# Storing the masked x^T phi(k) wv so that each product's 32 stationary columns are adjacent

## The chip, the core and the metric

The kernel runs on one core of a Trainium2 chip. Its engines are TensorE (PE in the profile; PEld is its weight load), VectorE (DVE), ScalarE (ACT), GpSimd (POOL) and SyncE (SP), which issues most DMAs. The metric is the device time of one execution in microseconds.

## The reference

Two linear-attention blocks, A and B, read the same input `x` (2048 x 640) with weights of their own, and a sigmoid gate per row mixes their outputs. There are 32 heads of 20 columns.

```python
qkv = (x @ wqkv) split into q, k, v, each (32 heads, 2048, 20)
phi = lambda t: jnp.where(t > 0, t + 1, jnp.exp(t)) + 1e-6
pq, pk = phi(q), phi(k)
kv  = einsum("bhsd,bhse->bhde", pk, v)
z   = einsum("bhsd->bhd", pk)
num = einsum("bhqd,bhde->bhqe", pq, kv)
den = einsum("bhqd,bhd->bhq", pq, z)[..., None] + 1e-6
block = (num / den, heads side by side) @ wo
g   = sigmoid((x * gate_w).sum(-1))
out = g * block_A + (1 - g) * block_B
```

## The kernel before

The kernel does not form v. Since kv = phi(k)^T x wv, it first computes G = x^T phi(k) (640 x 640), then wv^T G for four heads at a time, keeps what belongs to equal heads, and multiplies that by wo. The result is a matrix M per block (640 x 640), with which the output is phi(q) M, summed over both blocks after phi(q) has been scaled by gate and denominator.

The order of the work, all of it on TensorE with DVE and ACT behind:

- phi(k) of A in 16 row chunks (`k_chunk`, matmuls L205) mixed with half of phi(q) of A (`q_block`, L265), then the rest of phi(q) (`q_unit`, L254), the gate and the sums of phi(k).
- G of A (`g_pass`, L288, and `g_strassen`, L315), into the tiles `GT` (written by L285, L344, L332 and L362).
- phi(k) of B (16 chunks). After the second of them comes `kvt_pass(0)`: the 40 matmuls of wv^T G (`kvt_mm`, L396) and the masks (`kvt_mask`, L403) for A. After four of the later chunks DVE also takes a difference of rows (`p_diff`).
- phi(q) of B in ten units. `m_unit(0, c, "act")`, the wo product of A for one of five column sets c, stands after the first unit (c = 0), and in pairs after two later ones. Its matmuls are L429, and ACT copies the result to `M[0]` (L274).
- G of B, again by `g_pass` and `g_strassen`.
- The end, in an order written out by hand: `kvt_mm(1, kv, 0)`, `kvt_mask(kv, 0)`, `pairs[0].p1()` (five matmuls L515), `kvt_mm(1, kv, 1)`, `kvt_mask(kv, 1)`, row sums of phi(q) on DVE (`p_sums`, L454), `pairs[1].p1()`, and then the five wo products of B (L429) with sums of M on DVE between them (`m_sums`, L454).
- The output in eight pairs of row tiles (`Pair`, seven products in place of eight, matmuls L515, DVE additions L520), each stored by a DMA of SP.

Around the change: `KVT` holds, for each of four groups g, three stretches of 80 columns. The first and the third take the masked product of two sets of four heads; the middle one stays zero from a single memset (L105). `maskE` (80 x 80) is one where row and column belong to the same head. A wo product (`m_half`) runs four matmuls at a time, one for each g in its own 32 columns of the array (`tile_position`), for k = 0 and then k = 1. Its stationary operand has 80 rows and 32 columns: of two neighbouring stretches, every fifth column from c on (`mixed(heads, c)`). 16 of them come from masked data and 16 from zeros, so that k = 0 fills the first 16 rows of the result and k = 1 the last 16. In the order of memory the columns are thus 5 elements, 10 bytes, apart. Each `m_unit` has 16 such matmuls of 320 moving columns.

The code of these pieces runs under a manual schedule, so each engine's instructions stand in the order in which the program names them; the semaphores follow from which tile is read and written.

Of the kernel before, what the change touches and what calls it, by code (L numbers as in the profile page):

```python
# [8 lines left out]
P = 128  # L9
FP32 = mybir.dt.float32  # L10
BF16 = mybir.dt.bfloat16
ACT = mybir.ActivationFunctionType
ALU = mybir.AluOpType
# [3 lines left out]
DT = D // P  # L17
# [4 lines left out]
HF = D // 2  # L22
TW = 4
KG = 80
# [7 lines left out]
def kernel(  # L32
# [11 lines left out]
    nc = tc.nc  # L44
# [4 lines left out]
    persist = ctx.enter_context(tc.tile_pool(name="persist", bufs=1))  # L49
# [20 lines left out]
    pk = persist.tile([P, ST, D], BF16, name="pk")  # L70
    pqT = [persist.tile([P, DT, S], BF16, name=f"pqT{b}") for b in "AB"]
    GT = [persist.tile([P, DT, HF], BF16, name=f"GT{n}") for n in range(2)]
    KVT = persist.tile([P, 4, 3, KG], BF16, name="KVT")
    M = [persist.tile([P, DT, D], BF16, name=f"M{b}") for b in "AB"]
    wo_sb = [None, None]
    ident = persist.tile([P, P], BF16, name="ident")
# [2 lines left out]
    maskE = persist.tile([P, KG], BF16, name="maskE")  # L79
# [24 lines left out]
    nc.vector.memset(ones[:], 1.0)  # L104
    nc.vector.memset(KVT[:], 0.0)  # L105
    nc.vector.memset(lift[:], 1.0 + EPS)
# [22 lines left out]
    for n in range(1, NB):  # L129
        for c in range(DT):  # L130
            nc.sync.dma_start_transpose(
                out=xT[:, c, n * HB:(n + 1) * HB], in_=x2[n * HB:(n + 1) * HB, c * P:(c + 1) * P]
# [4 lines left out]
    for r in range(4):  # L137
        rows = slice(32 * r, 32 * r + 32)
        nc.gpsimd.tensor_copy(out=I4[rows], in_=ident[rows, rows])
    nc.gpsimd.tensor_copy(  # L140
        out=spread[:].rearrange("p (h t) -> p h t", t=TW), in_=I4[:, :, None].to_broadcast([P, H, TW])
    )
    nc.gpsimd.memset(maskE[:], 1.0)
    for sign, base in ((1, 0), (-1, Dh - 1)):
        nc.gpsimd.affine_select(
            out=maskE[:], in_=maskE[:], pattern=[[-sign * Dh, KG // Dh], [0, Dh]],
# [3 lines left out]
    for r in range(4):  # L150
        rows = slice(32 * r, 32 * r + 32)
        for sign, base in ((1, 0), (-1, Dh - 1)):
            nc.gpsimd.affine_select(
                out=E4[rows], in_=E4[rows], pattern=[[sign, D]],
# [89 lines left out]
    def mixed(t, m):  # L244

        return t[:, m::DT]
# [153 lines left out]

    def kvt_mask(pt, hf):

        nc.vector.tensor_tensor(  # L403
            out=KVT[:KG, 2 * hf:2 * hf + 2, 0:3:2, :],
            in0=pt[:KG, hf, 0:HF].rearrange("p (g k n) -> p g k n", g=2, k=2),
            in1=maskE[:KG, None, None, :].to_broadcast([KG, 2, 2, KG]), op=ALU.mult,
        )

    def kvt_pass(b):

        pt = ps("kvA")
        for hf in range(2):
            kvt_mm(b, pt, hf)
        for hf in range(2):
            kvt_mask(pt, hf)

    def m_unit(b, c, eng, pt=None):

        pt = ps("mA") if pt is None else pt
        for hf in range(2):  # L420
            m_half(b, c, hf, pt[:, hf, 0:HF])
        evac(M[b][:, c, :], pt, eng)

    def m_half(b, c, hf, dst):

        for k in range(2):
            for g in range(4):
                heads = KVT[:KG, g, k:k + 2, :].rearrange("p x n -> p (x n)")
                nc.tensor.matmul(  # L429
                    dst[32 * g:32 * g + 32, :], lhsT=mixed(heads, c),  # L430
                    rhs=wo_sb[b][:KG, 2 * g + k, hf * HF:(hf + 1) * HF], start=(k == 0), stop=(k == 1),
                    tile_position=(0, 32 * g),
                )
# [215 lines left out]
    for n in range(1, NB):  # L649
        nc.sync.dma_start(  # L650
            out=xn[:, n * CB:(n + 1) * CB, :], in_=x2[n * HB:(n + 1) * HB, :].rearrange("(q p) d -> p q d", p=P)
# [11 lines left out]
    with tc.manual_schedule():  # L663
# [32 lines left out]
        with late_pool("mid") as mid:  # L696
            first = bank(mid, "mid0", 2)
            kv = bank(mid, "mid1", 2)
            kvt_mm(1, kv, 0)
            kvt_mask(kv, 0)  # L700
            pairs[0].p1()
            kvt_mm(1, kv, 1)
            kvt_mask(kv, 1)
            p_sums(part[0], (1, 2))
            pairs[1].p1()
            m_unit(1, 0, "act", first)
            m_unit(1, 1, "act", bank(mid, "mid1", 2))
            m_sums((0, 1), (2, 1))
        with late_pool("single") as single:
            for hf in range(2):  # L710
                m_half(1, 2, hf, acc["z"][hf][:, 0:HF])
                nc.scalar.copy(out=M[1][:, 2, hf * HF:(hf + 1) * HF], in_=acc["z"][hf][:, 0:HF])
            m_sums((2,), (2, 1))
            m_unit(1, 3, "act", bank(single, "s3", 2))
            m_sums((3,), (2, 1))
            pts = [bank(single, f"s4{hf}")[:, 0:HF] for hf in range(2)]
            for hf in range(2):
                m_half(1, 4, hf, pts[hf])
            nc.scalar.copy(out=M[1][:, 4, 0:HF], in_=pts[0])
            nc.vector.tensor_copy(out=M[1][:, 4, HF:D], in_=pts[1])  # L720
            m_sums((4,), (2, 1))
# [16 lines left out]
        for i in range(1, half):  # L738
            p, after = pairs[i], pairs[i + 1] if i + 1 < half else None
# [53 lines left out]
```

## Time and profile before

| What | Value |
|---|---|
| time, median of 3 runs | 193.02 us (192.49 to 193.2) |
| the profiled execution's own time | 192.89 us |
| its span, first to last instruction | 191.0 us |
| granted TensorE clock, mean | 0.999 |
| PE busy | 186.5 us (98%), 1575 matmuls |
| PE weight loads busy | 125.7 us (66%), 1575 |
| DVE busy | 151.4 us (79%), 242 instructions |
| ACT busy | 70.1 us (37%), 98 instructions |
| wo products (L429) | 160 matmuls and as many weight loads: A at 100.0 to 100.8, 107.5 to 108.9 and 113.2 to 114.5 us, B at 147.7 to 150.6 us |
| masks (L403) | 4, of 80 x 320 elements; A at 78.25, B at 145.65 and 147.15 us |

A busy engine need not be the bound. Matmuls are pipelined, and their recorded lengths overlap, so the distance from one to the next says more than the busy time. A line of the timeline or of a group names start or busy time, the engine, the source line, the operation with output and inputs, and the shapes; square brackets give idle time before it and who ended it. The chain that ended last follows the execution back from its last instruction to what released it at each step.

### The profile page before, as it was taken

To read this page: it belongs to the slowest core of one execution; us is meant where nothing else is said; L and a number is where in the kernel's file an instruction comes from. 1 tells how busy PE (TensorE), PEld (TensorE's weight loads), DVE (VectorE), ACT (ScalarE), POOL (GpSimd) and SP (SyncE) were. 2 spreads that over 40 slices of the span, in tenths; PEclk is the share of its full clock that TensorE was granted. 3 is DMA by queue.
4 is the path that set the end of the run, shared out by engine and by line. 5 is a ranking of instruction groups with operands and counts; after the bars stand their busy time and mean duration, and the time that the engine had idled before them with its cause. 6 is when DMAs were issued, how large, how long until landed. Compare 5 with 4: busy or idle time off the path is not lost.

```text
span 191.0 us, 3771 instructions
## 1 busy us (share of the span) xinstructions
PE 186.5 (98%) x1575; PEld 125.7 (66%) x1575; DVE 151.4 (79%) x242; ACT 70.1 (37%) x98; POOL 8.5 (4%) x23
## 2 busy tenths in 40 slices
PE   8999999999999999999999999999999999999992
PEld 3666657765576677777765555576777776777771
DVE  1478868898998997789986785899797989787553
ACT  2055455555851501445453644511501611111110
POOL 8900000000000000000000000000000000000000
PEclk9999999999999999999999999999999999999999
DMA  5966439990050000410000007000000002312112
GB/s 184 315 138 93 93 73 350 318 257 9 2 172 3 0 0 0 122 53 0 3 0 0 3 2 169 6 0 0 3 0 0 3 0 95 114 69 72 69 69 70
DMA packets 18736, 14.00 MB, mean 73 GB/s; under 512 B 9376, under 2 KB 18720, under 8 KB 18720
## 3 DMA queue, kind: packets, MB, share of 16 engines
q1 hardware_dynamic: 18144, 13.11, 25.9%
q10 hardware_dynamic: 576, 0.66, 1.0%
q8 instruction: 12, 0.20, 0.5%
q14 instruction: 4, 0.03, 0.1%
HBM read 9.18 MB, written 2.62 MB: 62 GB/s over the span
## 4 chain that ended last, share of the span: by engine, by line
PE 92%; DVE 5%; issue 1%; ACT 0%; DVEq 0%; ACTq 0%
PE gs L315 13%; PE kA L205 12%; PE qB L254 12%; PE kB L205 11%; PE qA L254 7%; PE ox L515 5%; PE oy L515 5%; PE oz L515 5%; PE qA L265 5%; PE ow L515 2%; PE gB L288 2%; PE gA L288 2%; DVE pqTB L504 2%; PE warm L162 2%; PE mA L429 2%; DVE osb L520 1%
## 5 line engine op out<-in xcount | busy, mean ns | idle before, releaser
L205 PEld LDWEIGHTS <-xT 128*128 128x128 bf16 x320 | 31.2, 99 | 12.7 <-DVE xT L190 0.2
L198 DVE TENSOR_SCALAR e<-e 128x640 bf16<-128x640 bf16 (+1 forms) x52 | 18.7, 360 | 11.8 <-ACT e L195 11.3
L205 PE MATMUL kA<-wkA,xT 128*128 128x320 bf16 x160 | 23.2, 304 | 0.0
L254 PE MATMUL qB<-xT,wqB 128*128 128x512 bf16 x100 | 22.5, 380 | 0.0
L205 PE MATMUL kB<-wkB,xT 128*128 128x320 bf16 x160 | 22.1, 299 | 0.0
L195 ACT ACTIVATE e<-kB 128x640 bf16<-128x640 f32 x16 | 11.3, 704 | 20.7 <-PE kB L205 19.4
L254 PEld LDWEIGHTS <-wqB 128*128 128x128 bf16 x100 | 11.4, 118 | 9.7 <-issue 0.7
L195 ACT ACTIVATE e<-kA 128x640 bf16<-128x640 f32 x16 | 11.1, 704 | 13.2 <-PE kA L205 13.2
L195 ACT ACTIVATE e<-qB 128x1024 bf16<-128x1024 f32 x10 | 10.2, 1024 | 12.7 <-PE qB L254 12.7
L202 DVE SCALAR_TENSOR_TENSOR pk<-kA,e 128x640 bf16<-128x640 f32 x16 | 13.2, 824 | 1.7
L202 DVE SCALAR_TENSOR_TENSOR pk<-kB,e 128x640 bf16<-128x640 f32 x16 | 13.2, 824 | 1.7
L195 ACT ACTIVATE e<-qA 128x1024 bf16<-128x1024 f32 x10 | 10.2, 1024 | 10.6 <-PE qA L254 5.2
L254 PE MATMUL qA<-xT,wqA 128*128 128x512 bf16 x60 | 13.6, 380 | 0.0
L202 DVE SCALAR_TENSOR_TENSOR pqTB<-qB,e 128x1024 bf16<-128x1024 f32 x10 | 12.2, 1224 | 1.0
L315 PEld LDWEIGHTS <-xn 128*128 128x128 bf16 x96 | 9.1, 98 | 4.2 <-issue 0.8
L315 PEld LDWEIGHTS <-S 128*128 128x128 bf16 x96 | 9.4, 98 | 3.6
L552 ACT COPY u<-ox 128x320 f32<-128x320 f32 x8 | 3.4, 426 | 21.8 <-PE ox L515 21.8
L254 PEld LDWEIGHTS <-wqA 128*128 128x128 bf16 x60 | 6.9, 118 | 5.6 <-issue 0.3
L515 PEld LDWEIGHTS <-xT 128*128 128x128 bf16 x85 | 8.0, 98 | 3.1 <-DVE xT L454 0.2
L515 PEld LDWEIGHTS <-pqTA 128*128 128x128 bf16 x85 | 7.9, 98 | 2.9 <-issue 0.2
L515 PEld LDWEIGHTS <-pqTB 128*128 128x128 bf16 x80 | 7.8, 98 | 3.0
L538 ACT COPY p1s<-ox 128x320 f32<-128x320 f32 x8 | 3.4, 427 | 16.8 <-PE ox L515 16.8
(120 smaller groups left out, 288.3 us busy)
## 6 DMA issues: line engine op xcount, KB each, us to landing
out_dram<-osb SPq DMA_DIRECT2D x15, 160.0 KB, 1.8
xn<-in_A_x_dram SPq DMA_DIRECT2D x3, 640.0 KB, 6.4
wqA<-in_A_wqkv_dram SPq DMA_DIRECT2D x1, 800.0 KB, 6.9
wvA<-in_A_wqkv_dram SPq DMA_DIRECT2D x1, 800.0 KB, 9.9
woA<-in_A_wo_dram SPq DMA_DIRECT2D x1, 800.0 KB, 12.9
wkB<-in_B_wqkv_dram SPq DMA_DIRECT2D x1, 800.0 KB, 5.0
wqB<-in_B_wqkv_dram SPq DMA_DIRECT2D x1, 800.0 KB, 4.6
wvB<-in_B_wqkv_dram SPq DMA_DIRECT2D x1, 800.0 KB, 4.6
```

The costliest lines, as they stand in the source:

```text
L162: nc.tensor.matmul(warm[:, 0, :], lhsT=one_l, rhs=one_r, start=True, stop=True)
L195: nc.scalar.activation(out=e[:], in_=src, func=ACT.Exp)
L198: nc.vector.tensor_scalar(e[:], e[:], 1.0, EPS, op0=ALU.min, op1=ALU.add)
L202: nc.vector.scalar_tensor_tensor(out=dst, in0=src, scalar=1.0 + EPS, in1=e[:], op0=ALU.add, op1=ALU.max)
L205: nc.tensor.matmul(pt[:, hf, 0:HF], lhsT=xT[:, c, i * P:(i + 1) * P], rhs=wk[b][:, c, hf * HF:(hf + 1) * HF], start=(c == 0), stop=(c == D ...
L254: nc.tensor.matmul(pt[:, u, :], lhsT=mixed(wq[b][:, c, :], m), rhs=xT[:, c, n * HB:(n + 1) * HB], start=(c == 0), stop=(c == DT - 1),)
L265: nc.tensor.matmul(pt[:, u, :], lhsT=mixed(wq[b][:, c, :], m + u), rhs=xT[:, c, n * HB:(n + 1) * HB], start=(c == 0), stop=(c == DT - 1),)
L288: nc.tensor.matmul(pt[:, hf, 0:HF], lhsT=xn[:, i, c * P:(c + 1) * P], rhs=pk[:, i, hf * HF:(hf + 1) * HF], start=(i == 0), stop=(i == ST - 1),
L315: nc.tensor.matmul(pt[:, n, 0:HF], lhsT=left[:, i, n * P:(n + 1) * P], rhs=right[:, i, :], start=(first and i == 0), stop=(i == hc - 1), s ...
L429: nc.tensor.matmul(dst[32 * g:32 * g + 32, :], lhsT=mixed(heads, c), rhs=wo_sb[b][:KG, 2 * g + k, hf * HF:(hf + 1) * HF], start=(k == 0), ...
L504: nc.vector.tensor_tensor(out=pqT[b][:, m, :], in0=pqT[b][:, m, :], in1=rec, op=ALU.mult)
L515: nc.tensor.matmul(dst, lhsT=left[:, c, r0:r0 + P], rhs=right[:, c, :], start=(first and c == 0), stop=(c == DT - 1), skip_group_check=not ...
```

## The change

`KVT` gets a different order of columns: for each g and each c, the 16 columns of the first stretch with that c, then 16 zeros, then the 16 of the third stretch. The 32 stationary columns of a wo product are then side by side. The number of elements is the same, and so is the memset.

The masks write into that order. A mask instruction used to cover two groups and two head sets (2 x 2 x 80 columns); now there is one for each head set (2 x 16 x 5), so that a block has four masks instead of two. Each reads the product from PSUM in order and stores 5 successive elements 48 elements (96 bytes) apart before it moves on by one element. The wo products keep their number, shape and order. Two semaphore waits change in block B: the matmuls of `kvt_mm(1, kv, 1)` wait for the second piece of the first mask, and among the first wo product's weight loads the one for g = 2 now waits twice, for k = 0 on the first piece of the second mask and for k = 1 on its second piece.

```diff
-    KVT = persist.tile([P, 4, 3, KG], BF16, name="KVT")
+    KVT = persist.tile([P, 4, DT, 3, KG // DT], BF16, name="KVT")
...
     def kvt_mask(pt, hf):
-        nc.vector.tensor_tensor(
-            out=KVT[:KG, 2 * hf:2 * hf + 2, 0:3:2, :],
-            in0=pt[:KG, hf, 0:HF].rearrange("p (g k n) -> p g k n", g=2, k=2),
-            in1=maskE[:KG, None, None, :].to_broadcast([KG, 2, 2, KG]), op=ALU.mult,
-        )
+        src = pt[:KG, hf, 0:HF].rearrange("p (g k x c) -> p g k x c", g=2, k=2, c=DT)
+        mask = maskE[:KG].rearrange("p (x c) -> p x c", c=DT)[:, None].to_broadcast([KG, 2, KG // DT, DT])
+        for k in range(2):
+            nc.vector.tensor_tensor(
+                out=KVT[:KG, 2 * hf:2 * hf + 2, :, 2 * k, :].rearrange("p g c x -> p g x c"),
+                in0=src[:, :, k], in1=mask, op=ALU.mult,
+            )
...
     def m_half(b, c, hf, dst):
         for k in range(2):
             for g in range(4):
-                heads = KVT[:KG, g, k:k + 2, :].rearrange("p x n -> p (x n)")
+                rows = KVT[:KG, g, c, k:k + 2, :].rearrange("p y x -> p (y x)")
                 nc.tensor.matmul(
-                    dst[32 * g:32 * g + 32, :], lhsT=mixed(heads, c),
+                    dst[32 * g:32 * g + 32, :], lhsT=rows,
                     rhs=wo_sb[b][:KG, 2 * g + k, hf * HF:(hf + 1) * HF], start=(k == 0), stop=(k == 1),
                     tile_position=(0, 32 * g),
                 )
```

## The prediction

> **What bounds the kernel now.** I began with the page's busy times and the chain that ended last, to see whose time the span is.
>
> ```profile
> PE 186.5 (98%) x1575; PEld 125.7 (66%) x1575; DVE 151.4 (79%) x242; ACT 70.1 (37%) x98; POOL 8.5 (4%) x23
> PE 92%; DVE 5%; issue 1%; ACT 0%; DVEq 0%; ACTq 0%
> ```
>
> TensorE (PE) carries 92% of the chain and VectorE (DVE) 5%. The edit touches both: the weight loads of the wo product (L429) and the DVE masks that write KVT (L403). So I asked whether either lies on that chain. This is the chain in order of time, around the masks of block B (start, length, what):
>
> ```profile
> 143.80 1.13 DVE pqTB L504
> 144.93 0.80 DVE GT L362 x2
> 145.73 0.41 DVE KVT L403
> 146.14 0.04 issue
> 146.18 0.93 PE mid L396 x20
> 147.11 0.68 PE ox L515 x5
> 147.79 0.26 PE mid L429
> ```
>
> The first mask of block B is on the chain: PE sits idle until it ends and begins L396 again at 146.18, 0.05 us later. The second mask is not: PE goes from L515 straight to L429. Next, the groups with different shapes kept apart (busy, mean ns):
>
> ```profile
> L429 PEld LDWEIGHTS <-KVT 80*32 80x32 bf16 x160 | 4.9, 120 | 1.4 <-issue 1.1
> L370 PEld LDWEIGHTS <-ones 128*32 128x32 bf16 x64 | 1.6, 97 | 0.8 <-issue 0.4
> L332 DVE TENSOR_TENSOR GT<-gs,u 128x640 bf16<-128x640 f32 x2 | 1.6, 816 | 0.0
> L362 DVE TENSOR_TENSOR GT<-gs,u 128x320 bf16<-128x320 f32 x4 | 1.8, 480 | 0.0
> L520 DVE TENSOR_TENSOR osb<-oz,u 128x160 bf16<-128x160 f32 x4 | 1.2, 318 | 0.1
> L403 DVE TENSOR_TENSOR KVT<-mid,maskE 80x320 bf16<-80x320 f32 x2 | 1.0, 482 | 1.0 <-PE mid L396 1.0
> ```
>
> A weight load of 32 columns takes 120 ns where the columns lie 10 bytes apart (KVT) and 97 ns where they are side by side (ones). Whether those 23 ns reach the matmuls is seen in the PE timeline, in which all these groups are 32 matmuls of 320 columns, four at a time:
>
> ```profile
> 98.94 1.27 PE L370 MATMUL zB<-pk,ones 128*32 128x320 bf16 x32
> 107.49 1.37 PE L429 MATMUL mA<-woA,KVT 80*32 80x320 bf16 x32
> 113.23 1.30 PE L429 MATMUL mA<-woA,KVT 80*32 80x320 bf16 x32
> 147.72 1.29 PE L429 MATMUL mid<-woB,KVT 80*32 80x320 bf16 x32
> ```
>
> Eight rounds take 1.27 us with adjacent columns, 1.29 to 1.37 with strided ones. If every load were exposed, eight rounds would differ by 8 x 0.023 = 0.18; they differ by 0.02 to 0.03 in two of three places. So the loads are hidden except in one round after PE turns from 128-column to 32-column work. The turn itself, a gap of about 0.10 us, is the same for both: a qB matmul starts at 98.63 before the ones and at 107.18 before KVT, and the next work follows 0.31 later each time. Last, the DVE timeline:
>
> ```profile
> 78.25 0.88 DVE L403 TENSOR_TENSOR KVT<-kvA,maskE 80x320 bf16<-80x320 f32 x2
> 79.97 0.33 DVE L198 TENSOR_SCALAR e<-e 128x640 bf16<-128x640 bf16 x1 [0.84 <-ACT e L195]
> 145.65 0.48 DVE L403 TENSOR_TENSOR KVT<-mid,maskE 80x320 bf16<-80x320 f32 x1
> 147.15 0.49 DVE L403 TENSOR_TENSOR KVT<-mid,maskE 80x320 bf16<-80x320 f32 x1 [1.01 <-PE mid L396]
> 147.55 0.81 DVE L454 TENSOR_TENSOR pqTA<-pqTA,pqTB 128x1280 bf16<-128x1280 bf16 x1
> ```
>
> Two masks follow each other by 0.40 us, and after those of block A DVE is idle for 0.84.
>
> **Part 1, weight loads.** The 160 loads and matmuls stay the same in number and order; only the distance between the columns falls. What can be won is the excess over 1.27: 0.03 (at 113.23), 0.02 (at 147.72), and of the 0.10 at 107.49, where a second unit starts over in mid-row, I take two exposed rounds, 0.05. The unit at 100.04 follows the zB matmuls with no turn between them, so its loads are covered. Gain 0.10 us, bounds 0 and 0.15 (the whole excess). Most of it is in block A's units, which lie on the chain too (PE qB, mA, qB follow each other there).
>
> The Trainium skill, "TensorE: Matmul & The Clock Gate", section "LDWEIGHTS (loading the stationary operand)", prices a load by its number of columns alone, about 27 ns for 32 of them. By it the layout gains nothing and the sum below would be +0.07; the 97 and 120 ns above, at the same number of columns, do not agree with it.
>
> **Part 2, masks of block A.** Each of two masks of 320 elements becomes two of 160. From 640 to 320 elements the rows fall by 816 - 480 = 336 ns, 1.05 ns an element; a piece of 160 is then 0.48 - 0.17 = 0.31 us (the 128x160 row says 0.318), and the next one starts 0.40 - 0.17 = 0.23 after it. Four pieces take 3 x 0.23 + 0.32 = 1.01 instead of 0.88. The 0.13 us goes into the 0.84 idle that follows: nothing. Without that cover it would delay phi of a key chunk by 0.13. The KVT columns are needed only at 100.04.
>
> **Part 3, first mask of block B.** In the built order of the changed kernel the L396 matmul that waits for the mask waits for the second piece. That piece starts at 145.65 + 0.23 and ends at 146.20, not 146.13: +0.07 us on the chain. Behind that waiting matmul stands all of PE's remaining work, so nothing absorbs it.
>
> **Part 4, second mask of block B.** All times now lie 0.07 later: pieces start at 147.22 and 147.45, end at 147.54 and 147.77. The matmuls with k=0 need the first piece, those with k=1 the second: the changed order has one more wait, on the load for g=2, k=1, with all later matmuls queued behind it. Round one starts at 147.72 + 0.07 = 147.79; round two 0.15 later, its loads 0.10 before, at 147.84. The second piece is seen at 147.77 + 0.05 = 147.82. So the new wait costs nothing, with 0.02 us to spare; a piece that is x longer costs nearly x here. Starting on the first piece earlier gains nothing, since L515 sets the start. DVE's next work, the row sums from 147.55, starts 0.13 later; the timeline has it wait 0.27 us for ScalarE at 149.84 and 0.76 at 155.32, which take that up.
>
> **The unknown: storing at a distance.** The pieces write 5 elements 96 bytes apart, then step to the next 2 bytes. No DVE row of this trace stores like that. Below, a gain is excluded: every row here that reads f32 from PSUM goes at 1.05 ns an element or slower, contiguous as it is. Above: the nearest row is the strided load, 23 ns more for 32 elements, 0.7 ns an element, 0.11 us a piece. A doubling, 1.05 ns an element, is 0.17 us a piece. I take no surcharge, since these rows already spend a full element time where packed bf16 (L454, 320 elements in 0.317 us) is faster, but the ends go into the range.
>
> **Sum.** +0.07 - 0.10 = -0.03 us. The profiled execution took 192.89 us (span 191.0 and 1.9 around it, unchanged), so 192.86. The median shown is 193.02, 0.13 above that execution: 193.0.
>
> **Rivals.**
> *1, slower: scattered stores hold up the pieces.* Place: the two masks of block B. A surcharge of s per piece delays the first mask by 2s and the second piece again by about 2s, since PE waits for both; in block A 4s is hidden up to 0.7 us. The time is 192.99 + 4s: at s = 0.11 it is 193.4, at s = 0.17 it is 193.7, and from s = 0.25 (1.5 element times extra, 2.5 in all) it passes +1.0 us, 0.5%, which is about what a measurement of this kernel can tell from no change. For it: no row shows such a store, and the strided load pays. Against it stands the argument above, that the PSUM source already sets a slow pace. A price like the load's leaves the time within 0.5%.
> The Trainium skill, "Advanced Engine Details and Errata", section "SBUF Cachelines", says that SBUF is kept in 16-byte lines and that accesses which each go to another line are slower; the pieces do just that, and the rule speaks against this change. It gives no figure, and no DVE row here shows it.
> *2: the weight loads do not shorten, or it does not reach the matmuls.* Then only the +0.07 stays: 193.1. Against it stands the 97 against 120 ns.
> *3, faster: the adjacent columns also take away the gap at each turn.* Three turns of 0.10 and their rounds of 0.10 give -0.4, less the 0.07: 192.7. Even with the whole idle 0.31 us before 146.18 gone it stays under 1.0. The zB rows, with adjacent columns and the same gap, speak against it.
>
> **Chances.** Forecast 0.55; rival 1 with s up to 0.25 0.18, with more 0.18; rival 2 0.04; rival 3 0.05. Within 0.5% lie forecast, the cheap form of rival 1 and rival 2, 0.77, less a little that the spread of the runs (192.49 to 193.2) carries over either edge: 0.76. Slower 0.19, faster 0.05. The range goes from 192.4 (rival 3 with that spread) to 194.1 (rival 1 at s = 0.25 and the spread), and leaves out the dear form of rival 1.
>
> **What would show it.** Right: KVT loads at about 97 ns; L429 rows of 32 at 1.27 to 1.28; masks x4 and x4 at about 0.32 us, 0.23 apart; L396 restarting near 146.25; L429 in block B 0.15 after its first round. Wrong: masks of 0.45 us or more, a PE gap inside the first L429 rounds of block B, DVE busy without a break to 155, or PE gaps among the key chunks after 79.

## The result, and the profile after

The changed kernel is slower: 195.71 us median (194.74 to 196.38, 5 runs) against 193.1 us (192.49 to 193.43, 5 runs). The ratio is 1.0139, with a 95% interval of 1.0112 to 1.0167. The prediction was 193.0 with a range up to 194.1, so it missed. The profiled execution of the changed kernel took 194.74 us (span 192.9), the fastest of its five: its work up to the first wv^T G product ended 0.71 us earlier than in the profiled execution of before, although nothing differs there. To compare stages I therefore take the distance between two events inside one execution: from the first matmul of the wv^T G product of A (L396, kvA) to the first L515 product behind the wo products of B. Before, that is 150.57 - 76.14 = 74.43 us; after, 152.50 - 75.43 = 77.07. The stage has grown by 2.64, the medians by 2.61: the whole loss is in it. What follows it, up to the start of the last matmul, takes 36.69 us in both. The probe p1 below runs the same work as the kernel of before up to there, and its stage is 151.56 - 77.12 = 74.44, so the distance repeated within 0.01 us.

The busy times and the chain of the page after:

```profile
PE 186.4 (97%) x1575; PEld 124.2 (64%) x1575; DVE 155.4 (81%) x246; ACT 70.0 (36%) x98; POOL 8.5 (4%) x23
PE 78%; DVE 18%; issue 1%; ACT 1%; DVEq 0%; ACTq 0%
```

PE is as busy as before, DVE 4.0 us busier, and DVE's share of the chain has gone from 5% to 18%. The groups of the changed kernel, shapes kept apart, show what became of the loads and the masks:

```profile
L431 PEld LDWEIGHTS <-KVT 80*32 80x32 bf16 x160 | 4.3, 96 | 2.9 <-issue 1.1 <-DVE KVT L406 0.9
L406 DVE TENSOR_TENSOR KVT<-mid,maskE 80x160 bf16<-80x160 f32 x4 | 3.2, 984 | 1.0 <-PE mid L396 1.0
L406 DVE TENSOR_TENSOR KVT<-kvA,maskE 80x160 bf16<-80x160 f32 x4 | 3.0, 1045 | 0.0
```

The weight loads fell to 96 ns as forecast. A mask of half the elements takes about 1.0 us where a whole one took 0.48. The chain after, around the masks of block B:

```profile
145.65 1.50 DVE KVT L406 x2
...
147.19 0.94 PE mid L396 x20
...
148.16 1.61 DVE KVT L406 x2
...
149.81 1.13 PE mid L431 x26
```

The first mask holds the chain for 1.50 us where it held it for 0.41. The second mask, which was not on it because its 0.49 us lay behind L515, now holds it for 1.61. Block A is in the timelines of DVE and PE:

```profile
77.53 3.03 DVE L406 TENSOR_TENSOR KVT<-kvA,maskE 80x160 bf16<-80x160 f32 x4
80.19 0.52 DVE L198 TENSOR_SCALAR e<-e 128x640 bf16<-128x640 bf16 x1
```

```profile
98.22 1.13 PE L370 MATMUL zB<-pk,ones 128*32 128x320 bf16 x27
99.75 0.43 PE L370 MATMUL zB<-pk,ones 128*32 128x320 bf16 x5 [0.39 <-DVE pk L202]
```

Four masks take 3.03 us instead of 0.88, and the 0.84 us of idle DVE behind them is gone. At 99.75, 19 us later, the sums of phi(k) stop for the last key chunk: from first kvA to last zB matmul it is now 24.46 us instead of 23.77, +0.69. In between, the chain no longer lies on PE (before, 19.02 us of `kB` L205) but on DVE, from the masks to the last `pk`:

```profile
77.62 2.95 DVE KVT L406 x4
...
98.87 0.84 DVE pk L202
99.75 0.43 PE zB L370 x5
```

Most of DVE's new share of the chain is this stretch: the masks themselves are 3% of the span, and the rest is work on the key chunks that was not on the chain before.

### The profile page after: what moved, and what is told of

Same layout as the page of the kernel before. It is cut to its first block, busy times and chain, and to the rows that moved or that the text cites. A ratio compares the mean times of both kernels' runs of the same rounds, so it can differ in the third digit from the quotient of the medians.

```text
span 192.9 us, 3775 instructions
## 1 busy us (share of the span) xinstructions
PE 186.4 (97%) x1575; PEld 124.2 (64%) x1575; DVE 155.4 (81%) x246; ACT 70.0 (36%) x98; POOL 8.5 (4%) x23
## 4 chain that ended last, share of the span: by engine, by line
PE 78%; DVE 18%; issue 1%; ACT 1%; DVEq 0%; ACTq 0%
PE gs L315 13%; PE kA L205 11%; PE qB L254 10%; PE qA L254 7%; DVE pk L202 6%; PE oy L517 5%; PE oz L517 5%; PE ox L517 5%; PE qA L265 4%; DVE KVT L406 3%; PE ow L517 2%; PE gB L288 2%; PE gA L288 2%; DVE e L198 2%; DVE pqTB L506 2%; PE warm L162 2%
## 5 line engine op out<-in xcount | busy, mean ns | idle before, releaser
L205 PEld LDWEIGHTS <-xT 128*128 128x128 bf16 x320 | 31.0, 98 | 12.5 <-DVE xT L190 0.5
L198 DVE TENSOR_SCALAR e<-e 128x640 bf16<-128x640 bf16 (+1 forms) x52 | 19.1, 368 | 10.5 <-ACT e L195 10.1
L205 PE MATMUL kA<-wkA,xT 128*128 128x320 bf16 x160 | 22.6, 299 | 0.1
L205 PE MATMUL kB<-wkB,xT 128*128 128x320 bf16 x160 | 22.1, 299 | 0.0
```

The lines of the kernel that those rows point to most:

```text
L198: nc.vector.tensor_scalar(e[:], e[:], 1.0, EPS, op0=ALU.min, op1=ALU.add)
L205: nc.tensor.matmul(pt[:, hf, 0:HF], lhsT=xT[:, c, i * P:(i + 1) * P], rhs=wk[b][:, c, hf * HF:(hf + 1) * HF], start=(c == 0), stop=(c == D ...
```

## The experiments

Theory 1 is that the stores cost: each 2-byte store 96 bytes from the last. A piece then follows the one before by 0.72 us instead of 0.23 (3.03 = 3 x 0.72 + 0.87), s = 0.49 us in the prediction's terms. The rivals were the number of instructions and waits (A), the short inner runs of five (B), scatter on any side (C), and the place of the loss (D). "Stage" is the distance defined above, from each kernel's profiled execution; 74.43 before, 77.07 after.

**e1: the split alone.**

```diff
-            out=KVT[:KG, 2 * hf:2 * hf + 2, 0:3:2, :],
...
+        for k in range(2):
+            nc.vector.tensor_tensor(
+                out=KVT[:KG, 2 * hf:2 * hf + 2, 2 * k, :],
...
```

Expected:

> The layout of before, but each mask of 320 elements cut into two of 160, as in the changed kernel; stores stay side by side. Theory 1 (each 2-byte store that goes to a place 96 bytes from the last one costs about 0.003 us more, 0.49 us a piece): pieces of 0.31 us, 0.23 apart; only the split is paid, 0.07 us before the second wv^T G product of block B and up to 0.06 after it, so 0 to +0.15 us against before, ratio 1.000 to 1.001. Rival A (the cost is one of the number of instructions and of the extra wait): the whole +2.6 us, ratio 1.014.

Measured: 193.02 us, ratio 0.9998 (0.9971 to 1.0024), stage 74.50, +0.07. Its masks:

```profile
L405 DVE TENSOR_TENSOR KVT<-mid,maskE 80x160 bf16<-80x160 f32 x4 | 1.1, 313 | 1.0 <-PE mid L396 1.0
```

Pieces of 0.313 us, and the 0.07 that the prediction had for the split. Rival A falls.

**e2: the changed layout, stored in order.** The edit is against the changed kernel.

```diff
-        src = pt[:KG, hf, 0:HF].rearrange("p (g k x c) -> p g k x c", g=2, k=2, c=DT)
-        mask = maskE[:KG].rearrange("p (x c) -> p x c", c=DT)[:, None].to_broadcast([KG, 2, KG // DT, DT])
+        src = pt[:KG, hf, 0:HF].rearrange("p (g k x c) -> p g k c x", g=2, k=2, c=DT)
+        mask = maskE[:KG].rearrange("p (x c) -> p c x", c=DT)[:, None].to_broadcast([KG, 2, DT, KG // DT])
...
-                out=KVT[:KG, 2 * hf:2 * hf + 2, :, 2 * k, :].rearrange("p g c x -> p g x c"),
-                in0=src[:, :, k], in1=mask, op=ALU.mult,
+                out=KVT[:KG, 2 * hf:2 * hf + 2, :, 2 * k, :], in0=src[:, :, k], in1=mask, op=ALU.mult,
```

Expected:

> The layout of the changed kernel, four masks per block, but each mask runs over c outside and x inside: it stores runs of 16 adjacent elements (32 bytes) and reads the product from PSUM, and the mask, five elements apart. Theory 1 (the scattered stores cost): pieces near 0.31 us, time within 0.3 us of before. Rival B (short inner runs cost, whichever side is scattered; 32 runs of 5 in the changed kernel, 10 runs of 16 here): about a third of the 0.49 us a piece, 0.15, so 0.46 us pieces and +0.5 us. Rival C (any scattered side costs the same, reads too): pieces 0.72 us apart and +2.6 us as in the changed kernel.

Measured: 193.23 us, ratio 1.0017 (0.9992 to 1.0042), stage 74.43.

```profile
L406 DVE TENSOR_TENSOR KVT<-mid,maskE 80x160 bf16<-80x160 f32 x4 | 1.1, 316 | 1.0 <-PE mid L396 1.0
```

The same elements go to the same places, in another order, and a piece takes 0.316 us. Reads of PSUM five elements apart cost 3 ns a piece here. Rivals B and C fall; this loop order alone takes the loss back. Against e1, which has strided weight loads, the stage is 0.07 shorter: that is what the adjacent columns win.

**e3 and e4: one block at a time.** The scattered masks and the new layout for block A alone (`if b == 0`) or block B alone (`if b == 1`), with KVT cleared by GpSimd between the blocks.

> Block A has the changed kernel's layout and scattered masks, block B those of before; GpSimd, which is idle, clears KVT once more between the two. Theory 1 with its places: block A's four pieces take 3.0 us of DVE instead of 0.9; the key chunks behind them end later, and the sums of phi(k) (the ones products) wait about 0.6 us for the last chunk: +0.5 to +0.7 us, ratio 1.003. Rival D (block A is hidden, as the prediction had it, and the whole loss is in block B): 0 to -0.1 us.

> Block A has the layout and masks of before, block B the changed kernel's; GpSimd clears KVT once more between the two. Theory 1 with its places: the product after the first mask waits 1.09 us more, the wo product of block B 0.9 us more: +2.0 us, ratio 1.010. Rival D (the whole loss is in block B): +2.6 us, ratio 1.014. The sum of this and of the kernel with block A alone should be the whole loss.

Measured: A alone 193.56 us, ratio 1.0033 (1.0009 to 1.0057), stage 75.06, +0.63. B alone 194.74 us, ratio 1.0103 (1.006 to 1.0146), stage 76.44, +2.01. The sum, 2.64, is the whole loss. Rival D falls: block A is not hidden.

**p1: the stores by themselves.** Behind the work of the kernel of before stand groups of four DVE instructions that differ in the places of their stores only.

```python
for _ in range(4):
    tt(out=view(48, 1), in0=src, in1=mk, op=ALU.mult)
```

The first number of `view` is the distance between successive stores, in elements.

> The kernel of before, with groups of four DVE instructions (and four of ScalarE) put behind its last work; each multiplies 160 f32 elements of PSUM by the mask into a tile that is no longer needed, and only the places of the stores differ. Its total time says nothing. Theory 1 in its line form (stores that go to a new 16-byte stretch each time cost, as the Trainium skill has it): four instructions in 1.0 us with adjacent stores and with runs of five; little more at distances of 4 and 8 bytes; 3.0 us (0.72 apart) at 16, 32 and 96 bytes. Theory 1b (any gap between stores costs): 3.0 us from 4 bytes on. Theory 1c (the cost grows with distance): 16 and 32 bytes lie between. If stores are the limit, a bf16 source from SBUF with stores 96 bytes apart takes the same 3.0 us, and so do 4-byte stores 96 bytes apart unless the half word is what costs; runs of 16 with scattered reads take 1.0 us, as in the kernel that stored in order. ScalarE: open.

From the groups of that run, shapes kept apart (busy, mean ns). L781 stores side by side, L783 in runs of five, L785 at 4 bytes, L787 at 8, L789 at 16, L791 at 32, L793 at 96; L795 stores f32 at 96 bytes, L797 reads bf16 from SBUF and stores at 96 bytes, L799 stores runs of 16 and reads five apart:

```profile
L797 DVE TENSOR_TENSOR D<-TM,maskE 80x160 bf16<-80x160 bf16 x4 | 3.5, 868 | 0.1
L793 DVE TENSOR_TENSOR D<-oz,maskE 80x160 bf16<-80x160 f32 x4 | 3.5, 866 | 0.1
L789 DVE TENSOR_TENSOR D<-oz,maskE 80x160 bf16<-80x160 f32 x4 | 3.4, 860 | 0.1
L791 DVE TENSOR_TENSOR D<-oz,maskE 80x160 bf16<-80x160 f32 x4 | 3.4, 846 | 0.1
L787 DVE TENSOR_TENSOR D<-oz,maskE 80x160 bf16<-80x160 f32 x4 | 2.0, 508 | 0.1
L795 DVE TENSOR_TENSOR D<-oz,maskE 80x160 f32<-80x160 f32 x4 | 1.9, 472 | 0.1
L785 DVE TENSOR_TENSOR D<-oz,maskE 80x160 bf16<-80x160 f32 x4 | 1.3, 332 | 0.1
L783 DVE TENSOR_TENSOR D<-oz,maskE 80x160 bf16<-80x160 f32 x4 | 1.3, 323 | 0.1
L799 DVE TENSOR_TENSOR D<-oz,maskE 80x160 bf16<-80x160 f32 x4 | 1.3, 320 | 0.1
L781 DVE TENSOR_TENSOR D<-oz,maskE 80x160 bf16<-80x160 f32 x4 | 1.3, 317 | 0.1
```

So neither the short run nor a gap of 4 bytes costs; 8 bytes cost 0.19 us a piece, and at 16, 32 and 96 bytes it is 0.53 to 0.55, (866 - 317) / 160 = 3.4 ns an element. For 2-byte stores that fits the line form of theory 1, though not as a fixed price for each 16-byte stretch: at 4, 8 and 16 bytes the 160 stores touch about 40, 80 and 160 of them and cost 15, 191 and 543 ns. The source does not matter (L797). My guess that 4-byte stores would pay the same did not hold: at 96 bytes they take 0.155 us more than 2-byte stores side by side, under a third (4-byte stores side by side were not measured). So the width of the store counts as well as the distance; why is open. Four instructions took 1.37 us, not 1.0, even side by side: each here overwrites what the last one stored, which may be why they do not overlap, but that was not tested; the differences are what counts. ScalarE, storing at 96 bytes, took 3.57 us for four, as DVE did; it had no group with adjacent stores to compare with.

**e8 and e9: another way to adjacent columns.** The wv^T G product reads its moving columns five apart, so that its result already has the order of KVT, and KVT alternates 17 stretches of zeros and data, so that one mask stores a half. e9 adds a PSUM tile for each half in block B.

```diff
...
-                    rhs=GT[hf][:, c, j * KG:(j + 1) * KG], start=(c == 0), stop=(c == DT - 1),
+                    rhs=GT[hf][:, c, j * KG:(j + 1) * KG].rearrange("p (x c) -> p c x", c=DT), start=(c == 0), stop=(c == DT - 1),
...
```

> Adjacent stationary columns without scattered stores and without the split: the wv^T G product reads its moving columns five apart, so that it leaves PSUM already in the order of KVT; KVT holds for each column set 17 stretches of 16 columns, zeros and data in turn, so one mask of 320 elements stores all, in runs of 32 bytes. Theory 1: masks 0.48 us, weight loads 97 ns, the wo products won 0.10 us and nothing lost: -0.1 us, ratio 0.999 to 1.000. Rival E (moving columns 10 bytes apart slow the 80 small products): each of them takes longer than its 38 ns, up to double, +1.5 us for block A's 40 and as much for block B's, ratio up to 1.015.

> As the kernel with the permuted product, and in block B the two halves of the wv^T G product get a PSUM tile each, so that the second half no longer waits for the first mask. Theory 1: the 0.31 us of idle PE before the second half goes too, together -0.4 us, ratio 0.997 to 0.999. Rival F (the wait only moves to the wo product behind the second mask): -0.1 us.

Measured: e8 196.94 us, ratio 1.0198 (1.0171 to 1.0226); e9 197.35 us, ratio 1.0228 (1.0196 to 1.0261). The PE timeline of e8:

```profile
76.00 3.77 PE L396 MATMUL kvA<-GT,wvA 128*80 128x80 bf16 x40
79.59 2.85 PE L205 MATMUL kB<-wkB,xT 128*128 128x320 bf16 x10
```

40 products take 3.59 us where they took 77.67 - 76.14 = 1.53: 90 ns each against 38. (The granted clock was 0.95 in this stretch; at 1.0, the first 20 of block B take 149.72 - 147.94 = 1.78 us, 89 ns each.) Rival E was right, by more than its bound. Of the idle PE that e9 was to win, the slower product had already taken most: DVE is done with its earlier work when the product ends, so L515 covers nearly all of the first mask, and the second half starts 150.48 - 149.72 = 0.76 us after the start of L515 in e8 against 0.70 in e9. But e9 lost more elsewhere. Its fourth wo product stops:

```profile
154.25 1.27 PE L430 MATMUL s<-woB,KVT 80*32 80x320 bf16 x32 [0.30 <-ACT MB L274]
```

It starts 154.25 - 153.23 = 1.02 us after the third one, in e8 0.54. So a wait did move, as rival F has it, though to another place.

**e10: one mask, read scattered, stored in order.** KVT as in e8, the product as before:

```diff
...
+            out=KVT[:KG, :, 8 * hf + 1:8 * hf + 8:2, :].rearrange("p c j x -> p j c x"),
+            in0=pt[:KG, hf, 0:HF].rearrange("p (j x c) -> p j c x", j=4, c=DT),
...
```

> The wv^T G product as before (its moving columns side by side). KVT holds 17 stretches of 16 columns for each column set, and one mask of 320 elements reads PSUM five elements apart and stores runs of 32 bytes. Theory 1 (only scattered stores cost; reads of PSUM five apart were 0.314 against 0.310 us a piece): masks 0.48 us, loads 97 ns, 0.10 us won at the wo products, no split to pay: -0.1 us against before, ratio 0.999 to 1.000. Rival C (scattered reads cost when the instruction is long): masks over 0.6 us, +0.2 us or more.

Measured: 192.9 us, ratio 1.001 (0.9988 to 1.0032), masks 494 to 498 ns (477 to 482 before), stage 74.36. The stage agrees with theory 1 (-0.07), and the runs can't tell 0.07 us from nothing. It has what the change was built for, without its cost.

**e11, e12 and e13: the idle PE at the first mask.** e11 is e10 with a PSUM tile for each half of the product in block B; e12 has these tiles alone; e13 is e11 with the tiles of the last two wo products exchanged.

```diff
...
-            kv = bank(mid, "mid1", 2)
...
+            kvs = [bank(mid, f"mid{n}", 2) for n in range(2)][::-1]
...
+            first = bank(mid, "mid1", 2)
...
-            m_unit(1, 1, "act", bank(mid, "mid1", 2))
+            m_unit(1, 1, "act", bank(mid, "mid0", 2))
```

> The same, and in block B a PSUM tile for each half of the wv^T G product, so that the second half waits for the first L515 product only and not for the first mask. Theory 1: the 0.31 us of idle PE ahead of it goes and nothing later takes it up, since the second mask has its own cover of L515: -0.4 us, ratio 0.997 to 0.999. Rival F (the wait only moves behind the second mask): as the kernel with one mask in order, -0.1 us.

> The kernel of before with the own PSUM tiles alone: layout, masks and strided weight loads as before. Theory 1: -0.3 us, ratio 0.998 to 0.999. Rival F: 0.

Measured: e11 192.88 us, ratio 1.0 (0.9978 to 1.0021), stage 74.54; e12 193.18 us, ratio 1.0024 (1.0004 to 1.0043), stage 74.65. The gap before the second half is gone in both (in e11 it starts 0.68 us after the start of L515, before 0.99), and nothing was won. The PE timeline of e11 says where it went, to the place where e9 lost its time:

```profile
149.43 1.27 PE L430 MATMUL s<-woB,KVT 80*32 80x320 bf16 x32 [0.30 <-ACT MB L274]
```

The fourth wo product takes over the banks of the second one, which ScalarE has not copied out yet; before, these were the banks of the first one. It starts 149.43 - 148.41 = 1.02 us after the third, before 0.54: 0.48 lost against 0.31 won. The wait moved, as rival F has it, though not behind the second mask. e13 allocates the last product's tiles ahead of the fourth's:

> As the kernel with one mask in order and own tiles, with the PSUM tiles of the last two wo products exchanged: the fourth product now reuses the banks of the first one and not of the second, whose copy by ScalarE ends 0.6 us later. Theory 1: the 0.47 us gap before the fourth product goes, the gap before the second wv^T G half stays away; against before -0.4 us, ratio 0.997 to 0.999. Rival F (the time is taken up later once more, by DVE's sums ahead of L515): no difference from before.

Measured: 192.47 us, ratio 0.9976 (0.9954 to 0.9999), stage 150.85 - 76.80 = 74.05, -0.38. Both gaps are gone. It is the one version here whose interval lies below the kernel of before, by a quarter of a per cent and only just; most of the 0.38 is from a wait that the change under study did not touch.

## Why the prediction was wrong

- **What bounds the kernel** was read rightly: PE, with the first mask of block B on the chain. The stage that grew holds all that the change touches.
- **Part 1, weight loads**: forecast 0.10 us, measured 0.07 (e1 against e2, and again e10 against before). The loads fell to 96 ns, and two of the three rows of 32 matmuls to 1.27 us, as named in advance (113.17 in the changed kernel, 147.50 in e2). The row with a turn in its middle went from 1.37 to 1.34 only, 0.03 where the sum had 0.05, so the rest of its excess was not the loads.
- **Part 2, block A**: this step failed. It set the masks' extra time against one idle spell of 0.84 us and, in rival 1, called 0.7 us of it hidden, with no price for the rest. The masks cost 3.03 - 0.88 = 2.15 us more. What the idle spell did not take stayed as a lag of 0.94 us (the last `pk` starts 98.87 - 75.43 = 23.44 us after the first kvA, before 98.64 - 76.14 = 22.50) through 14 key chunks, in which DVE has no other long break, and 0.69 of it came out at the sums of phi(k). Alone it costs +0.63 (e3). With the forecast's own pieces the step held: in e1 the split goes into the idle spell, which falls from 0.84 to 0.71.
- **Parts 3 and 4** had the right places. The split costs +0.07 (e1). The new waits on both pieces then each take two surcharges: 1.50 - 0.41 = 1.09 at the first mask and, with the stage's second part, 2.01 in all (e4).
- **The unknown** is the step that was mis-sized, and it decides the miss. I took no surcharge and had 0.17 us a piece as its upper end; it is 0.49. The nearest row, a strided weight load, was a read by another engine, and a doubling of the element time was a guess. The argument that a PSUM source leaves the stores time to spare was wrong: the source does not matter (p1), and 3.4 ns an element is three element times on top of one.
- **Rival 1** was the mechanism, with its place in block B. Put in s = 0.49, its sum gives 192.99 + 1.96 = 194.95; the 0.69 of block A that it left out makes 195.64, against 195.71. It had 0.36 in all, but the range ended at s = 0.25 and left out its dear form. With a store pattern that no row showed and a rule against it, the range should have held the dear form.
- The Trainium skill, "Advanced Engine Details and Errata", "SBUF Cachelines", has the 16-byte line as the unit and asks for two accesses to a line. The runs fit that unit for 2-byte stores: the cost is flat from 16 bytes on (860, 846 and 866 ns). At 8 bytes, two stores to a line, 0.19 us a piece is left, so two are not quite enough here.
- **The signs of being wrong**: two of the four showed, masks of 1.0 us and the PE gap of 0.40 us inside the first wo product of block B (before 149.81). PE had no gap among the key chunks, as block A's delay came out behind them, and DVE paused for 0.26 us before 151.75.

## What to carry to other kernels

A change of layout that helps the reader moves the scatter to the writer, so price the writer's store pattern first: scattering on the read side, with stores in runs, gave the same layout for nothing here. If no row shows the pattern, don't bound it by a row of another engine or direction; spend one probe on it. A delay on a busy engine is not hidden by the idle spell behind it unless that spell is as long as the delay: follow the lag to the next place where someone waits for that engine. And when medians spread by half a per cent, the distance between two events inside the execution shows a tenth of a microsecond (74.43 and 74.44 for the same work in two runs here).

## What the runs showed of the hardware

- DVE stores of 2 bytes: 160 elements in 317 ns side by side, 332 at 4 bytes, 508 at 8, 846 to 868 from 16 to 96 bytes; f32 at 96 bytes 472. L198 right behind block A's masks is recorded with 0.52 us instead of 0.33, but it starts 0.37 us before the last mask's record ends, so it is not shown to be slower.
- Reading PSUM five f32 apart costs DVE nearly nothing (0.316 us against 0.310 to 0.313 for 160 elements, 0.494 to 0.498 against 0.477 to 0.482 for 320).
- Moving columns 10 bytes apart take PE from 38 to 90 ns for a product of 80 columns, where stationary columns 10 bytes apart take a load of 32 columns from 96 ns (e2) to 119 (e1), of which 0.07 us in 160 loads reaches the time.
- A turn from 128-column to 32-column work costs PE about 0.1 us with either layout of the weights: two qB matmuls of 512 columns start 0.22 us apart, and the first wo product behind them 0.31 us after the last (107.18 to 107.49 before, 107.15 to 107.46 after).
